# Later W_q loads and folds, earlier v tiles and warming on a constant in a fused attention and GEGLU kernel

## The chip, the cores and the metric

The kernel runs on one core of one Trainium2 chip. The metric is the time of the device for one execution, in microseconds (us); the median of several runs is given with the lowest and the highest. TensorE is PE, its weight loads are PEld, VectorE is DVE, ScalarE is ACT, GpSimd is POOL, and SyncE is SP, which issues all DMA transfers of this kernel. Each engine works through its own queue in order.

## What is computed

Two blocks follow each other on one sequence of 2048 rows of width 640. The first is linear attention with 32 heads of width 20 and a learned feature map; the second is a gated feed-forward layer of width 1536. Cut to what matters:

```python
x = A_x                                     # (1, 2048, 640), bf16
qkv = layernorm(x) @ wqkv                   # q, k, v: 32 heads of 20
pq, pk = q @ w_phi[h], k @ w_phi[h]         # per head, 20 x 20
phi_q = concat(softmax(pq), softmax(-pq))   # 40 features
phi_k = concat(softmax(pk), softmax(-pk))
kv, z = phi_k.T @ v, sum(phi_k)
o = (phi_q @ kv) / (phi_q @ z + 1e-6)
h = x + o @ wo
out = h + (gelu(layernorm(h) @ w_gate) * (layernorm(h) @ w_up)) @ w_down
```

## The kernel before

The 2048 rows are 16 tiles of 128 rows, in four blocks of four (`x_sb[0]` to `x_sb[3]`). The width of 640 is five chunks of 128 (`NC`). The order of every engine's instructions is written out by hand; the program's order is the queue's order.

**Folding.** `w_phi` is multiplied into W_k and W_q once, so that k and q come out of the projections ready for the exponentials. W_k and W_q are loaded transposed (`load_T`, five DMA transposes each, line 187, into `WkT` and `WqT`). `bd` builds `BD`, a block-diagonal form of `w_phi`, from the tile `wphi` and a mask on DVE (line 389). `fold` (lines 215 to 240) multiplies one 128-row chunk after the other, six matmuls each (tile `wa`), and copies each result out of PSUM: by ACT where the chunk is in `KA` (for W_k) or `QA` (for W_q), otherwise by DVE.

**Layernorm.** `ln_st` takes a tile's statistics on DVE (line 110); the reciprocal standard deviation comes from ACT (tiles 0 to 2, `log=True`) or from POOL (lines 122 and 123). `ln_ap` applies it on DVE or ACT. The result must be transposed into `LN1T`: with `on_pe` by five PE transposes and a copy out of PSUM by ACT or DVE (`ln_tp`, line 148), otherwise by a DMA transpose on SP's queue (line 150). Tiles 0 and 1 are only centred at first (`ln_0`, tile `xc`), and their scale is applied when v and k are read out; their full layernorm is made up for at tile 10 of the loop. Tile 3's statistics are two ACT passes with running sums (`st3_act`) and five small POOL steps.

**Start.** `warm` runs matmuls on a zeroed tile (line 211) while the first loads are on their way: nine of 512 columns, and two more behind the first transposes. Then v of tiles 0 to 2 is built in pieces (`v_part`, line 291), as the chunks of W_v land; the folds of W_k, v of tile 3 and the transposes of tiles 3 and 4 follow.

**Loop over the tiles t.** `k_tile` does k's ten matmuls (line 275, 320 columns each) and two exponentials on ACT (tile `E`, line 308). Until the end of the tiles, `v_mm(t + 4)` and `v_ev(t + 4)` do v of four tiles on, `ln_ap(t + 6)` the layernorm of six tiles on, and `k_norm` sums, inverts and scales on DVE and POOL (tiles `sk`, `rs`, `vt`). `kv_tile` (line 341) adds phi_k.T @ v of finished tiles into one PSUM tile, in the groups of `KVG`. `FQ` says at which t each chunk of W_q is folded. At t = 15 the q projection begins (`q_mm`, line 363), and from there attention, the output projection and the feed-forward layer run with q's remaining work between them.

**PSUM.** The big tiles (`gtile`) share four buffers of two banks; from t = `T3` there are three, the fourth goes to `kvp`.

Of the kernel before, what the change touches and what calls it, by code (L numbers as in the profile page):

```python
# [8 lines left out]
BF16 = mybir.dt.bfloat16  # L9
F32 = mybir.dt.float32  # L10
ALU = mybir.AluOpType
ACTF = mybir.ActivationFunctionType
# [5 lines left out]
def kernel(  # L18
# [12 lines left out]
    nc = tc.nc  # L31
    P = 128
    S = 2048
    D = 640
# [3 lines left out]
    NT = S // P  # L38
    NB = NT // 4
    NC = D // P  # L40
    NF = FF // P
    EPS = 1e-5
    HD = D // 2

    H0 = [(P * c) // Dh for c in range(NC)]
    NH = [(P * c + P - 1) // Dh - H0[c] + 1 for c in range(NC)]
    NWARM = 9
    VP = (0, 2, 4, 6, 9, 11)
    KA, QA = (1,3), (0,1,2,3,4)
    FQ = (4, 5, 6, 7, 8)  # L50

    QG = ((0, 1), (2, 3), (4, 5), (6,), (7, 8), (9, 10), (11, 12), (13, 14), (15,), (16,), (17,), (18,), (19,))
    QT = (15, 15, 15, 15)
    WA = 2
    T3 = 4

    KVG = {5: (0, 1), 9: (2, 3, 4, 5), 13: (6, 7, 8, 9), 15: (10, 11)}
    VC = Dh + 1
# [6 lines left out]
    x_v = A_x.rearrange("b (p t) d -> p (b t) d", t=NT)  # L65
# [23 lines left out]
    nhalf = const.tile([P, 2], F32, name="nhalf")  # L89
# [10 lines left out]
    def gtile(name):  # L100
        return psG.tile([P, 2, 512], F32, name=name, tag="G")
# [74 lines left out]
    nc.sync.dma_start(Wv[:, 0:2, :], w_v[:, 0:2, 2 * D:3 * D])  # L176
    nc.sync.dma_start(x_sb[0][:, 2:3, :], x_v[:, 2:3, :])
    nc.sync.dma_start(Wv[:, 2:4, :], w_v[:, 2:4, 2 * D:3 * D])
    nc.sync.dma_start(wphi, phi_v.rearrange("(c p) f -> p c f", p=P))
    nc.sync.dma_start(Wv[:, 4:5, :], w_v[:, 4:5, 2 * D:3 * D])  # L180
    nc.sync.dma_start(x_sb[0][:, 3:4, :], x_v[:, 3:4, :])
    nc.sync.dma_start(x_sb[1][:, 0:2, :], x_v[:, 4:6, :])

    def load_T(WT, i, *ds):

        for d in ds:
            nc.sync.dma_start_transpose(WT[:, :, d * P:(d + 1) * P], A_wqkv[d * P:(d + 1) * P, i * D:(i + 1) * D])  # L187
# [4 lines left out]
    wu_v = B_w_up.rearrange("(c p) n -> p c n", p=P)  # L192


    zero = fp.tile([P, 512], BF16, name="zero")
    nc.vector.memset(zero, 0.0)
    for i in range(8):
        nc.vector.memset(vS[i][:, :, Dh], 1.0)
    make_identity(nc, ident)
# [6 lines left out]
                                compare_op=ALU.is_ge, fill=0.0, base=Dh - 1 - off, channel_multiplier=-1)  # L206

    wu = gtile("wu")
    def warm(n):
        for _ in range(n):  # L210
            nc.tensor.matmul(wu[:, 0, :], lhsT=zero[:, 0:P], rhs=zero, start=True, stop=True)

    warm(NWARM)

    def fold(WT, W2, halves, ds=range(NC)):

# [37 lines left out]
    def ln_st(*tiles, act=True, between=None, log=False):  # L254
        for t, v in zip(tiles, ln_stats(p1, [x_sb[t // 4][:, t % 4, :] for t in tiles], "1", act, between, log)):
            lnp[t] = v

    def ln_ap(t, on_act=False, on_pe=False):
        ln = (ln_act if on_act else ln_dve)(p1, "1", *lnp[t])
        if on_pe:  # L260
            lnp[t] = ln
        else:
            transpose_to(LN1T[t // 4][:, :, t % 4 * P:(t % 4 + 1) * P], ln, False)

    def ln_tp(t, on_dve=False):
        transpose_to(LN1T[t // 4][:, :, t % 4 * P:(t % 4 + 1) * P], lnp[t], True, on_dve)

    def lnT(t, c):
        b, tl = divmod(t, 4)
        return LN1T[b][:, c, tl * P:(tl + 1) * P]  # L270

    def proj(ps, t, W, us=(0, 1)):
        for u in us:
            for c in range(NC):
                nc.tensor.matmul(ps[:, u, 0:HD], lhsT=lnT(t, c), rhs=W[:, c, u * HD:(u + 1) * HD],  # L275
                                 start=(c == 0), stop=(c == NC - 1))

    pv = {}

    def v_mm(t, us=(0, 1)):  # L280
        if 0 in us:
            pv[t] = gtile("pv")
        proj(pv[t], t, Wv, us)

    def v_part(t, *cs):

        if 0 in cs:
            pv[t] = gtile("pv")
        for c in cs:
            for u in range(2):  # L290
                nc.tensor.matmul(pv[t][:, u, 0:HD], lhsT=lnT(t, c), rhs=Wv[:, c, u * HD:(u + 1) * HD],
                                 start=(c == 0), stop=(c == NC - 1))

    def v_ev(t):
        nc.scalar.activation(vS[t % 8][:, :, 0:Dh].rearrange("p (u h) f -> p u h f", u=2),
                             pv[t][:, :, 0:HD].rearrange("p u (h f) -> p u h f", f=Dh), ACTF.Copy,
                             scale=lnp[t][2] if t in CT else 1.0)
# [4 lines left out]

    def k_tile(t):
        pk = gtile("pk")
        proj(pk, t, Wk2)
        Ek[t] = ev.tile([P, 2, D], BF16, name="E", bufs=8)
        for s in range(2):
            nc.scalar.activation(Ek[t][:, s, :].rearrange("p (u f) -> p u f", u=2), pk[:, :, 0:HD],  # L308
                                 ACTF.Exp, scale=((lnp[t][2], nrstd[t]) if t in CT else (1.0, -1.0))[s])
# [60 lines left out]
    def st3_act(i):  # L370

        xt = x_sb[0][:, 3, :]
        nc.scalar.activation(sq3, xt, (ACTF.Square, ACTF.Identity)[i], accum_out=sm3[:, i:i + 1])
        if i == 1:
            nc.gpsimd.tensor_scalar(v3[:, 0:1], sm3[:, 1:2], sm3[:, 1:2], -1.0 / (D * D), op0=ALU.mult, op1=ALU.mult)
            nc.gpsimd.tensor_scalar_add(v3[:, 0:1], v3[:, 0:1], EPS)
            nc.gpsimd.tensor_scalar(v3[:, 1:2], sm3[:, 0:1], 1.0 / D, v3[:, 0:1], op0=ALU.mult, op1=ALU.add)
            nc.gpsimd.tensor_tensor(v3[:, 2:3], v3[:, 1:2], nhalf[:, 0:1], op=ALU.pow)
            nc.gpsimd.tensor_scalar(v3[:, 3:4], sm3[:, 1:2], 1.0 / D, None, op0=ALU.mult)
            lnp[3] = xt, v3[:, 3:4], v3[:, 2:3], None  # L380

    sq3 = fp.tile([P, D], BF16, name="sq3")
    sm3 = fp.tile([P, 2], F32, name="sm3")
    v3 = fp.tile([P, 4], F32, name="v3")

    def bd(c0, c1):

        n = c1 - c0
        nc.vector.tensor_tensor(BD[:, c0:c1], wphi[:, c0:c1, None, :].to_broadcast([P, n, 8, Dh]),
                                hmask[:, c0:c1, :, None].to_broadcast([P, n, 8, Dh]), ALU.mult)  # L390
# [4 lines left out]
    xc = [ln_0(t) for t in CT[:1]]  # L395
    tr_c(0)
    xc.append(ln_0(1))
    warm(WA)
    ln_st(2, act=False, log=True)
    v_part(0, 0, 1)  # L400
    tr_c(1)
    st3_act(0)
    v_part(0, 2, 3)
    bd(0, 3)
    ln_ap(2, on_pe=True)
    bd(3, NC)
    st3_act(1)
    v_part(1, 0, 1, 2, 3)
    ln_tp(2, True)
    v_part(0, 4)  # L410
    v_ev(0)
    ln_st(4, act=False)
    ln_ap(3, on_pe=True)
    v_part(1, 4)
    v_ev(1)
    v_part(2, *range(NC))
    v_ev(2)
    nc.sync.dma_start(x_sb[1][:, 2:4, :], x_v[:, 6:8, :])
    nc.sync.dma_start(x_sb[2], x_v[:, 8:12, :])
    nc.sync.dma_start(x_sb[3], x_v[:, 12:16, :])  # L420
    fold(WkT, Wk2, False, (0, 1, 2))
    ln_tp(3, False)
    fold(WkT, Wk2, False, (3, 4))
    v_mm(3)
    v_ev(3)
    ln_ap(4, on_pe=True)
    ln_tp(4)
    ln_st(5, act=False)
    ln_st(6)
    ln_ap(5, on_pe=True)  # L430
    ln_st(7)
    fp_cm.__exit__(None, None, None)
    ev_cm = tc.tile_pool(name="ev", bufs=1, side="right", reuse_waits="tile")
# [2 lines left out]
    for t in range(NT):  # L436
        if t == T3:
            ps_cm.close()
            psG = ps_cm.enter_context(tc.tile_pool(name="psG", bufs=3, space=PSUM, reuse_waits="tile"))
            psK = ps_cm.enter_context(tc.tile_pool(name="psK", bufs=1, space=PSUM, reuse_waits="tile"))  # L440
            kvp = psK.tile([P, 2, 512], F32, name="kvp")
        k_tile(t)
        if t == 0:
            ln_ap(6)
        if t in FQ:
            fold(WqT, Wq2, True, [i for i, f in enumerate(FQ) if f == t])
        for j in range(len(QT)):
            if t == QT[j]:
                q_mm(j)
                q_exp(j)  # L450
        for i in KVG.get(t, ()):
            kv_tile(i)
        if t + 4 < NT:
            v_mm(t + 4)
            if t == 0:
                ln_tp(5)
        if t > 0 and t + 6 < NT:
            ln_ap(t + 6, on_act=True)
        if t + 4 < NT:
            v_ev(t + 4)  # L460
        if t % 2 == 0 and t + 8 < NT:
            ln_st(t + 8, t + 9)
        k_norm(t)
        if t < NC:
            load_T(WqT, 0, t)
        if t == 10:

            for i in CT:
                ln_ap(i)
        if t == 9:  # L470
            nc.gpsimd.memset(KV, 0.0)
            nc.gpsimd.memset(kmask, 1.0)
            for r in HALF:
                nc.gpsimd.affine_select(out=kmask[r], in_=kmask[r], pattern=[[4, NC], [-Dh, 4]],
                                        compare_op=ALU.is_ge, fill=0.0, base=0, channel_multiplier=1)
                nc.gpsimd.affine_select(out=kmask[r], in_=kmask[r], pattern=[[-4, NC], [Dh, 4]],
                                        compare_op=ALU.is_ge, fill=0.0, base=Dh - 1, channel_multiplier=-1)
            nc.gpsimd.tensor_copy(KV[:, :, 0, :, KC - 1], kmask)
            nc.gpsimd.tensor_copy(KV[:, :, 1, :, 0], kmask)
        if t == 10:  # L480
            nc.sync.dma_start(Wg, wg_v)
            nc.sync.dma_start(Wo, wo_v)
            nc.sync.dma_start(Wu, wu_v)
# [328 lines left out]
```

## Time and profile before

| | |
|---|---|
| median of 3 runs | 278.56 us (277.83 to 278.84) |
| the profiled execution | 278.98 us |
| its span, first to last instruction | 277.1 us |
| PE busy | 271.7 us (98%) |
| DVE busy | 176.5 us (64%) |
| ACT busy | 138.9 us (50%) |
| POOL busy | 97.0 us (35%) |

The profile is one execution. All times in it count from the start of the span; the execution's own time is 1.9 us longer than the span. A row of the timeline is: start, time from the first start to the last end, engine, line, operation, what it writes and reads with sizes, how many instructions, and in square brackets how long the engine was idle before and what ended that. A busy PE isn't one at its peak: matmuls are pipelined, and the ends in the profile are modelled.

### The profile page before, as it was taken

What the parts mean: (1) busy time and instruction counts of PE and PEld (TensorE: products, weight loads), DVE (VectorE), ACT (ScalarE), POOL (GpSimd) and SP (SyncE); (2) the same over time, 40 slices, a digit from 0 to 9 for tenths busy, and PEclk for the clock granted to TensorE, in tenths of its full rate; (3) what the DMA queues carried; (4) which work ended last, traced back from release to release, by engine and by line L of the source; (5) the groups of instructions that cost most, each with busy time, mean ns of one, the idle gap of its engine ahead of it and who ended that gap; (6) DMA issues with size and microseconds to landing.
All of it is one profiled execution on the core that took longest, in us unless ns stands there. A gap on an engine that the chain in (4) does not pass through costs nothing.

```text
span 277.1 us, 5913 instructions
## 1 busy us (share of the span) xinstructions
PE 271.7 (98%) x2337; PEld 173.2 (62%) x2337; DVE 176.5 (64%) x337; ACT 138.9 (50%) x239; POOL 97.0 (35%) x221
## 2 busy tenths in 40 slices
PE   8999999999999999999999999999999999999995
PEld 3677777774655887788864555675555577444574
DVE  6699999899396786576467773346876433332322
ACT  4679989668597846365543354313245410223100
POOL 4337997774302216455403463102165300000000
PEclk9999999999999999999999999999999999999999
DMA  6964842289740021314111123110123211000011
GB/s 198 184 241 102 109 78 50 26 229 393 251 151 0 4 47 26 72 47 97 28 50 47 25 50 71 25 55 21 47 47 70 27 47 47 27 0 0 0 50 47
DMA packets 42235, 21.37 MB, mean 77 GB/s; under 512 B 35040, under 2 KB 40416, under 8 KB 42208
## 3 DMA queue, kind: packets, MB, share of 16 engines
q1 hardware_dynamic: 42208, 21.01, 30.8%
q8 instruction: 18, 0.29, 0.4%
q14 instruction: 9, 0.07, 0.1%
HBM read 10.18 MB, written 2.62 MB: 46 GB/s over the span
## 4 chain that ended last, share of the span: by engine, by line
PE 87%; SPq 4%; DMA 3%; DVE 2%; ACT 2%; issue 1%
PE gu L657 38%; PE pd L676 19%; PE pq L363 8%; PE po L600 8%; PE pk L275 5%; PE pv L275 4%; PE ab L528 3%; SPq L187 2%; PE kvp L341 2%; DMA LN1T<-ln 2%; DVE stats L110 1%; DMA WkT<-in_A_wqkv_dram 1%; ACT E L308 1%; ACT ln L134 1%; PE wa L229 1%
## 5 line engine op out<-in xcount | busy, mean ns | idle before, releaser
L660 ACT ACTIVATE g<-gu 128x512 bf16<-128x512 f32 (+1 forms) x60 | 30.7, 512 | 69.1 <-PE gu L657 68.2
L663 DVE TENSOR_TENSOR GT<-gu,g 128x512 bf16<-128x512 f32 (+1 forms) x60 | 34.3, 579 | 48.2 <-PE gu L657 39.3
L657 PE MATMUL gu<-LN2T,Wg 128*128 128x512 bf16 (+1 forms) x300 | 61.8, 337 | 0.1
L657 PE MATMUL gu<-LN2T,Wu 128*128 128x512 bf16 (+1 forms) x300 | 61.7, 336 | 0.0
L676 PE MATMUL pd<-Wd,GT 128*128 128x320 bf16 (+2 forms) x396 | 53.5, 295 | 0.0
L676 PEld LDWEIGHTS <-GT 128*128 128x128 bf16 x396 | 37.9, 98 | 14.7 <-DVE GT L663 0.2
L657 PEld LDWEIGHTS <-Wu 128*128 128x128 bf16 x300 | 29.4, 98 | 22.6
L657 PEld LDWEIGHTS <-Wg 128*128 128x128 bf16 x300 | 28.8, 98 | 21.4
L275 PEld LDWEIGHTS <-LN1T 128*128 128x128 bf16 x290 | 27.9, 98 | 10.9 <-DMA LN1T<-ln 0.3
L679 DVE TENSOR_TENSOR y<-pd,x_sb 128x320 bf16<-128x320 f32 (+2 forms) x29 | 13.9, 480 | 29.0 <-PE pd L676 29.0
L323 POOL TENSOR_TENSOR vt<-vS,rs 128x672 bf16<-128x672 bf16 x22 | 29.1, 1343 | 9.1 <-DVE rs L319 7.4
L600 PE MATMUL po<-Wo,oT 128*128 128x320 bf16 x160 | 24.4, 299 | 0.0
L275 PE MATMUL pk<-Wk,LN1T 128*128 128x320 bf16 x160 | 24.0, 299 | 0.0
L315 DVE TENSOR_REDUCE sk<-E 128x64 f32<-128x1280 bf16 x16 | 22.9, 1434 | 1.2 <-ACT E L308 1.2
L363 PE MATMUL pq<-LN1T,Wq 128*128 128x512 bf16 x100 | 22.9, 379 | 0.0
L368 ACT ACTIVATE Eq<-pq 128x1024 bf16<-128x1024 f32 (+1 forms) x26 | 19.9, 830 | 2.4 <-PE pq L363 2.4
L308 ACT ACTIVATE E<-pk 128x640 bf16<-128x640 f32 x28 | 18.3, 716 | 4.5 <-PE pk L275 4.3
L600 PEld LDWEIGHTS <-oT 128*128 128x128 bf16 x160 | 15.6, 98 | 7.4 <-ACT oT L148 0.3
L275 PE MATMUL pv<-Wv,LN1T 128*128 128x320 bf16 x130 | 19.8, 299 | 0.2 <-DMA LN1T<-ln 0.2
L577 DVE TENSOR_TENSOR tt<-AB,w 128x1280 bf16<-128x1280 f32 x12 | 17.9, 1488 | 1.1 <-POOL w L570 0.9
L134 ACT ACTIVATE ln<-x_sb,v,rstd 128x640 bf16<-128x640 bf16 x14 | 12.9, 920 | 10.7 <-POOL v L636 10.3
L363 PEld LDWEIGHTS <-Wq 128*128 128x128 bf16 x100 | 9.5, 98 | 10.4 <-issue 0.2
(112 smaller groups left out, 292.8 us busy)
## 6 DMA issues: line engine op xcount, KB each, us to landing
out_dram<-y SPq DMA_DIRECT2D x15, 160.0 KB, 1.8
Wg<-in_B_w_gate_dram SPq DMA_DIRECT2D x1, 1920.0 KB, 9.1
Wu<-in_B_w_up_dram SPq DMA_DIRECT2D x1, 1920.0 KB, 15.0
Wd<-in_B_w_down_dram SPq DMA_DIRECT2D x1, 1920.0 KB, 8.0
x_sb<-in_A_x_dram SPq DMA_DIRECT2D x2, 640.0 KB, 6.6
Wo<-in_A_wo_dram SPq DMA_DIRECT2D x1, 800.0 KB, 10.7
x_sb<-in_A_x_dram SPq DMA_DIRECT2D x4, 160.0 KB, 2.9
Wv<-in_A_wqkv_dram SPq DMA_DIRECT2D x2, 320.0 KB, 3.8
```

Of the source, the lines that this page charges most:

```text
L275: nc.tensor.matmul(ps[:, u, 0:HD], lhsT=lnT(t, c), rhs=W[:, c, u * HD:(u + 1) * HD], start=(c == 0), stop=(c == NC - 1))
L308: nc.scalar.activation(Ek[t][:, s, :].rearrange("p (u f) -> p u f", u=2), pk[:, :, 0:HD], ACTF.Exp, scale=((lnp[t][2], nrstd[t]) if t in C ...
L315: nc.vector.reduce_sum(sk, Ek[t].rearrange("p s (h f) -> p (s h) f", f=Dh), axis=AX.X)
L323: eng.tensor_tensor(vt[:, s], vS[t % 8], rs[:, s * H:(s + 1) * H, None].to_broadcast([P, H, VC]), ALU.mult)
L363: nc.tensor.matmul(pqs[j][:, i, :], lhsT=Wq2[:, kc, c * P:(c + 1) * P], rhs=LN1T[b][:, kc, :], start=(kc == 0), stop=(kc == NC - 1))
L368: nc.scalar.activation(Eq[j][:, :, s, :], pqs[j][:, 0:len(QG[j])], ACTF.Exp, scale=(1.0, -1.0)[s])
L577: nc.vector.tensor_tensor(tt.rearrange("p s (h f) -> p s h f", f=Dh), num, w[:, :, :, None].to_broadcast([P, 2, H, Dh]), ALU.mult)
L600: nc.tensor.matmul(pos[u], lhsT=st[t][:, c, :], rhs=Wo[:, c, u * HD:(u + 1) * HD], start=(c == 0), stop=(c == NC - 1))
L657: nc.tensor.matmul(gu[i][:, 0:n], lhsT=W[:, c, f * P:(f + 1) * P], rhs=LN2T[b][:, c, a0:a1], start=(c == 0), stop=(c == NC - 1))
L660: nc.scalar.activation(g[:, 0:n], gu[0][:, 0:n], ACTF.Gelu_apprx_tanh)
L663: nc.vector.tensor_tensor(st[b, "g", f][:, a0:a1], gu[1][:, 0:n], g[:, 0:n], ALU.mult)
L676: nc.tensor.matmul(ps, lhsT=st[b, "g", f][:, tl * P:(tl + 1) * P], rhs=Wd[:, f, f0:f1], start=(f == 0), stop=(f == NF - 1))
```

## The change

- Warming reads the constant 1.0 that the framework provides (a broadcast of one column) in place of a zeroed tile, so the memset goes. In front: seven matmuls of 512 columns and eight of 128 in place of nine of 512. Behind the first transposes: seven of 128 in place of two of 512.
- The load of tile 3's x stands ahead of `wphi` and of W_v's last chunk on SP's queue.
- `BD` is built in one piece, behind the layernorm of tile 2.
- Tile 3's statistics are the mean first and then the squares of the centred values; two POOL steps are left of five. Its layernorm (`ln_3`) stands behind the statistics of tile 4.
- The transposes of tiles 3 and 4 are copied out by DVE; those of tile 3 come ahead of the folds of W_k. v of tile 3 stands ahead of fold 3, v of tile 4 ahead of fold 4. ACT copies the chunks 0, 2 and 4 of W_k (before: 1 and 3).
- k of tile 0 takes the row chunks in the outer loop and the halves in the inner one.
- W_q is loaded at t = 7 to 10 in place of 0 to 4 and folded at t = 10 to 14 in place of 4 to 8.
- Three PSUM buffers from t = 3 in place of 4. The loads of Wg, Wo and Wu stand at t = 13 in the program in place of 10.

```diff
-    NWARM = 9
-    KA, QA = (1,3), (0,1,2,3,4)
-    FQ = (4, 5, 6, 7, 8)
+    KA, QA = (0, 2, 4), (0, 1, 2, 3, 4)
+    LQ = (7, 8, 9, 9, 10)
+    FQ = (10, 11, 12, 13, 14)
-    WA = 2
-    T3 = 4
+    T3 = 3
...
     nc.sync.dma_start(Wv[:, 2:4, :], w_v[:, 2:4, 2 * D:3 * D])
+    nc.sync.dma_start(x_sb[0][:, 3:4, :], x_v[:, 3:4, :])
     nc.sync.dma_start(wphi, phi_v.rearrange("(c p) f -> p c f", p=P))
     nc.sync.dma_start(Wv[:, 4:5, :], w_v[:, 4:5, 2 * D:3 * D])
-    nc.sync.dma_start(x_sb[0][:, 3:4, :], x_v[:, 3:4, :])
...
-    zero = fp.tile([P, 512], BF16, name="zero")
-    nc.vector.memset(zero, 0.0)
+    ones = nc.const_aps.tensor(1.0, [P, 512], BF16)
...
-    def warm(n):
-        for _ in range(n):
-            nc.tensor.matmul(wu[:, 0, :], lhsT=zero[:, 0:P], rhs=zero, start=True, stop=True)
-    warm(NWARM)
+    def warm(*cols):
+        for n in cols:
+            nc.tensor.matmul(wu[:, 0, 0:n], lhsT=ones[:, 0:P], rhs=ones[:, 0:n], start=True, stop=True)
+    warm(*[512] * 7, *[P] * 8)
...
-    def proj(ps, t, W, us=(0, 1)):
-        for u in us:
-            for c in range(NC):
+    def proj(ps, t, W, us=(0, 1), rows=False):
+        for u, c in sorted(((u, c) for u in us for c in range(NC)), key=lambda x: x[::-1] if rows else x):
...
-        proj(pk, t, Wk2)
+        proj(pk, t, Wk2, rows=t == 0)
...
-        nc.scalar.activation(sq3, xt, (ACTF.Square, ACTF.Identity)[i], accum_out=sm3[:, i:i + 1])
-        if i == 1:
...
+        if i == 0:
+            nc.scalar.activation(sq3, xt, ACTF.Identity, scale=-1.0 / D, accum_out=v3[:, 0:1])
+        else:
+            nc.scalar.activation(sq3, xt, ACTF.Square, bias=v3[:, 0:1], accum_out=v3[:, 1:2])
+            nc.gpsimd.tensor_scalar(v3[:, 2:3], v3[:, 1:2], 1.0 / D, EPS, op0=ALU.mult, op1=ALU.add)
+            nc.gpsimd.tensor_tensor(v3[:, 3:4], v3[:, 2:3], nhalf[:, 0:1], op=ALU.pow)
+
+    def ln_3():
+        ln = lnp[3] = p1.tile([P, D], BF16, name="ln1", bufs=3)
+        nc.vector.tensor_scalar(ln, x_sb[0][:, 3, :], v3[:, 0:1], v3[:, 3:4], op0=ALU.add, op1=ALU.mult)
...
-    warm(WA)
+    warm(*[P] * 7)
     ln_st(2, act=False, log=True)
     v_part(0, 0, 1)
     tr_c(1)
     st3_act(0)
     v_part(0, 2, 3)
-    bd(0, 3)
     ln_ap(2, on_pe=True)
-    bd(3, NC)
+    bd(0, NC)
     st3_act(1)
-    v_part(1, 0, 1, 2, 3)
+    v_part(1, 0, 1)
     ln_tp(2, True)
+    v_part(1, 2, 3)
     v_part(0, 4)
     v_ev(0)
-    ln_st(4, act=False)
-    ln_ap(3, on_pe=True)
     v_part(1, 4)
     v_ev(1)
+    ln_st(4, act=False)
+    ln_3()
+    ln_ap(4, on_pe=True)
     v_part(2, *range(NC))
     v_ev(2)
...
+    gtile('wu')
+    ln_tp(3, True)
     fold(WkT, Wk2, False, (0, 1, 2))
-    ln_tp(3, False)
-    fold(WkT, Wk2, False, (3, 4))
+    ln_tp(4, True)
     v_mm(3)
+    ln_st(5, act=False)
     v_ev(3)
-    ln_ap(4, on_pe=True)
-    ln_tp(4)
-    ln_st(5, act=False)
+    fold(WkT, Wk2, False, (3,))
+    v_mm(4)
+    ln_ap(5, on_pe=True)
+    fold(WkT, Wk2, False, (4,))
+    v_ev(4)
+    ln_tp(5)
     ln_st(6)
-    ln_ap(5, on_pe=True)
     ln_st(7)
...
-        if t + 4 < NT:
+        if 0 < t < NT - 4:
             v_mm(t + 4)
-            if t == 0:
-                ln_tp(5)
...
-        if t < NC:
-            load_T(WqT, 0, t)
+        load_T(WqT, 0, *[i for i, f in enumerate(LQ) if f == t])
...
-        if t == 10:
+        if t == 13:
             nc.sync.dma_start(Wg, wg_v)
```

## The prediction

> **What bounds the kernel now.** I read the page first, then the chain of waits in order of time, then the timeline of the first 70 us, engine by engine.
>
> ```profile
> span 277.1 us, 5913 instructions
> PE 271.7 (98%) x2337; PEld 173.2 (62%) x2337; DVE 176.5 (64%) x337; ACT 138.9 (50%) x239; POOL 97.0 (35%) x221
> PE 87%; SPq 4%; DMA 3%; DVE 2%; ACT 2%; issue 1%
> ```
>
> TensorE (PE) is the bound, and the change takes no real matmul away: the same projections, folds and transposes are in the program, only the warming differs. So all it can win is time in which PE waits. The chain shows where that is:
>
> ```profile
> 11.21 3.41 DMA WkT<-in_A_wqkv_dram
> 14.67 0.50 PE wa L229 x6
> ...
> 28.85 4.90 DMA LN1T<-ln
> 33.80 1.53 PE pv L275 x10
> 35.33 1.36 PE pk L275 x10
> 36.69 0.32 PE wa L229 x6
> ```
>
> After 33.80 us the chain is nearly all PE, to the end of the span. Before it, loads, VectorE (DVE) and ScalarE (ACT) take turns. The prices are in the chain too: ten 320-column matmuls (one v or k tile) 1.36 us, one fold 0.32, five transposes 0.28 (rows at 79.63 and 83.61). The timeline shows the start:
>
> ```profile
> 0.92 0.27 DVE L196 MEMSET zero<- 128x256 uint32 x1 [0.92 <-PEq L796]
> 1.25 4.02 PE L211 MATMUL wu<-zero 128*128 128x512 bf16 x9 [1.25 <-DVE zero L196]
> 4.22 0.39 DVE L251 TENSOR_SCALAR xc<-x_sb,mvc 128x640 bf16<-128x640 bf16 x1
> 5.06 0.74 PE L147 MATMUL tp<-ident,xc 128*128 128x128 bf16 x5
> ...
> 9.23 0.74 ACT L373 ACTIVATE sq<-x_sb 128x640 bf16<-128x640 bf16 x1 [1.56 <-DMA x_sb<-in_A_x_dram]
> 12.85 0.45 DVE L139 TENSOR_SCALAR ln<-x_sb,v 128x640 bf16<-128x640 bf16 x1 [1.58 <-POOL v L379]
> 16.73 1.52 PE L275 MATMUL pk<-Wk,LN1T 128*128 128x320 bf16 x10
> 19.44 0.44 PE L147 MATMUL tp<-ident,ln 128*128 128x128 bf16 x5
> ```
>
> The first tile, ready at 4.61, waits for warming until 5.06. ACT waits 1.56 us for x of tile 3; DVE, in order, waits 1.58 for GpSimd's (POOL's) chain on it. In the transposes, PE finishes at 19.72 (19.44 + 0.28) the following work: six tile transposes, five folds, v of tiles 0 to 4, k of tile 0. That is my yardstick.
>
> **Part by part: the start.** Warming on a constant: PE need not wait for the memset; ACT and DVE begin at 0.79 and 0.92, so PE at about 0.85 instead of 1.24. Nine matmuls in 4.02 us, less a tail of 0.18, are 427 ns each; a 128-column one is a quarter, 107. 7 x 0.427 + 8 x 0.107 = 3.85, so it ends at 4.70, and the first transposes come 0.36 earlier. Alone this wins nothing: the next wait is further down. The seven small ones behind them (0.75) end before ACT's copy, as the two big ones did (6.51 against 6.58).
>
> Loads: the DMA answers put the landings at 6.9 us (Wv chunks 2-3, L178), 8.07 (wphi, L179), 8.8 (Wv chunk 4, L180), 9.25 (x of tile 3, L181) and 10.0 (tiles 4-5, L182). x of tile 3 took 0.45 of the queue. Moved ahead of wphi it lands near 7.4, wphi near 8.55, Wv's chunk near 9.3; tiles 4-5, and the W_k transposes behind them on SP's queue, do not move.
>
> DVE: copy of tile 1 ends about 7.85, the layernorm of tile 2 now comes at once (to 8.32), then the whole BD when wphi is there: 0.66 + 0.48 less one overhead, 1.02, to 9.6. The copy of tile 2 is queued behind BD and ends at 10.14 (before: 9.74 + 0.49 = 10.23). So wphi's later landing eats the earlier start.
>
> Tile 3: ACT's two sums can start at 7.7 instead of 9.23 and end at 9.56. POOL's five steps (11.02 to 12.82) become two (0.27 and 0.57 with a gap), rstd at 10.6. DVE does the statistics of tile 4 first, to 11.27, and tile 3's layernorm from 11.3 to 11.75 instead of 12.85 to 13.30. Its wait of 1.58 is gone; a wait of 0.5 for tile 4's rstd comes in its place, with the copy of tile 3 queued behind it (12.73 to 13.22).
>
> PE then, in its new order: v of tile 2 from 10.2 to 11.56; transposes of tile 3 at 11.80; folds 0 to 2 to 13.04; transposes of tile 4 at 13.27 (a PSUM buffer must come free); v of tile 3 13.55 to 14.91; fold 3 to 15.23 (its weights landed at 13.8); v of tile 4 to 16.59; fold 4 to 16.91 (landed at 14.6, so that wait is covered); transposes of tile 5 wait for DVE until 17.10, to 17.38; k of tile 0 to 18.74. By row chunks it asks for the last W_k chunk after eight matmuls, at 18.47, when ACT has long copied it (17.8). Without that order it would wait 0.3. Against 19.72: **0.98 us**. Evacuating chunks 0, 2 and 4 on ACT instead of 1 and 3 gives DVE 0.78 back, its two extra transpose copies take 0.98; in sum DVE reaches the end of tile 6's statistics at 18.16 instead of 18.88.
>
> **Part by part: the loop.** W_q's loads leave tiles 0 to 4 and its folds leave tiles 4 to 8. There ACT is full:
>
> ```profile
> 39.89 1.31 ACT L308 ACTIVATE E<-pk 128x640 bf16<-128x640 f32 x2
> 40.07 1.52 PE L275 MATMUL pv<-Wv,LN1T 128*128 128x320 bf16 x10
> 41.05 0.73 ACT L238 CAST Wq<-wa 128x640 bf16<-128x640 f32 x1
> ```
>
> The E rows start 3.15 apart (36.73, 39.89, 43.03, 46.18), PE's matmuls need 2 x 1.36 + 0.32 = 3.04, and PE loses 0.19 at 39.88, 0.15 at 43.10, 0.09 at 45.96, and 0.17 at 33.63 to a transposed tile that landed 4.9 us after issue instead of the usual 2.6. Without the fold's copy (0.58 from its start at 41.05 to that of ACT's next row at 41.63) ACT needs 2.57 against PE's 2.72. **0.60 us** come back, if nothing takes their place. What could: (a) transposed tiles. ACT's ln ends about 2.2 after a k tile, landing 2.65 later; PE wants it at 5.44: 0.6 of room. (b) The W_q loads stand on SP's queue between the layernorm transposes of tiles 13 to 15 and those of tiles 0 and 1; at 1.28 each to issue and 3 to 4.6 to land, the last is there about 54, its fold at about 58. (c) The folds at tiles 10 to 14 meet an ACT without layernorms there: 1.2 + 0.6 against PE's 1.68, with room from the kv matmuls. (d) The first q matmuls follow the last fold by one k tile; its copy is done at about 60.1, wanted at 60.66. (e) Wg, Wo and Wu stand later in the program, but nothing is between on SP's queue and they wait for nothing, so they go out where they did. (f) Three PSUM buffers from tile 3 on: E of the tile before is read 1 us before its buffer is wanted. I cost (a) to (f) at nothing; bounds 0 and 0.3 in sum, from PE's stalls of 0.1 to 0.2 in the rows above.
>
> The chain that must keep up is k_norm's, DVE and POOL:
>
> ```profile
> 51.96 1.49 DVE L315 TENSOR_REDUCE sk<-E 128x64 f32<-128x1280 bf16 x1 [1.22 <-ACT E L308]
> 68.99 1.96 POOL L323 TENSOR_TENSOR vt<-vS,rs 128x672 bf16<-128x672 bf16 x1 [1.35 <-DVE rs L319]
> 69.34 2.48 PE L341 MATMUL kvp<-vt,E 128*64 128x84 bf16 x120
> ```
>
> POOL's last vt ends at 70.95; PE wants it five sixths into its six kv tiles, at 71.4. DVE is full from 20 to 50, then waits 1.22 for E of tile 10. With folds gone from the tiles before, that E comes over 3 us earlier, so the wait goes: 0.72 + 1.22 = 1.94 earlier for DVE, 1.58 for PE. It keeps up, by 0.8.
>
> **Sum.** 0.98 + 0.60 = 1.58 us. The profiled execution took 278.98, its span 277.1 and 1.9 around it; it would become 277.4. It lies 0.42 above the median of 278.56, so the median becomes 277.0. The start is worth 0.5 (wphi delayed by its own 1.17 instead of 0.45) to 1.3 (tiles 4-5 usable at 10.0, no buffer wait); the loop 0.3 to 0.9 (all of PE's gaps between 19.72 and 61.70: 41.05 us of matmuls in 41.98). So this case spans 0.8 to 2.2.
>
> The clock is the unknown. The warm rows run at 427 ns per 512 columns, and 512-column matmuls in steady state take 4.32/20 = 216: PE is at half speed until some point between 5.5 and 6.6.
>
> The Trainium skill (TensorE: Matmul & The Clock Gate, Part 1) says that the clock is released by a window of about 3.4 us of sustained activity that runs free of the kernel's start, and Part 4 that transposes do not count as activity in the same way. That speaks against replacing 1024 columns of warming behind the first transposes by 896. By it one window missed would cost up to half of 3.4, 1.7 us, where my sum has zero.
>
> **Rivals.** *The k_norm chain does not move* (DVE's early savings are lost): POOL ends at 70.95 less the 1.22, 69.7, and PE, there at 69.8, hardly waits; if the 1.22 is lost too, PE waits until 70.95 and keeps about 0.5: 278.1. For it: DVE at 97% from 15 to 50. Against: the wait of 1.22 is PE's doing.
>
> *The start is taken back*: BD, now one piece ahead of tile 2's copy on DVE, holds up every later copy; only the loop's 0.6 stays: 278.0. For it: wphi landed 4.9 after issue, the slowest per byte.
>
> *Slower: PE stays at half speed.* At half speed until a time t, PE loses half of what lies between 6.2 (its first v matmul) and t, less the 1.3 us that it idles between 6.2 and 10.2 in my schedule: (t - 6.2)/2 - 1.3. The 1.58 are gone at t = 12.0; from 14.7 the kernel is slower by over 0.5%; at 17, all of the start, 4.1 are lost against 1.58 won: 281.1. For it: less warming, and small pieces. Against: PE's gaps after 6.2 are hardly more than before, when it was at full speed from 6.6.
>
> *The change does not do what it says* for the weights' loads, (e) above, and that costs nothing either way.
>
> **Chances.** Forecast 0.66 (own range 276.4 to 277.8), the k_norm chain 0.12, the start taken back 0.12, slower 0.10. A measurement of this kernel tells 0.5%, 1.39 us, from no change. Below 277.17 lie four fifths of the forecast case: 0.52; above 279.95 0.10; the rest 0.38. The range runs from 276.0, the 276.4 with a little more from a clock released earlier, to 278.5, past the two middle rivals and a half-speed period.
>
> **What would show it.** Right: first transposes near 4.7; tile 3's layernorm near 11.3; k of tile 0 ends before 19; no PE gaps between tiles 4 and 9; DVE without a wait at tile 10; q matmuls from near 60.1. Wrong: tile 2's copy later than 10.5, v matmuls at 270 ns after 7 us, PE waiting for vt at the last kv tiles, for W_q's last copy, or for a transposed tile.

## The result and the profile after

The changed kernel takes 277.56 us (277.19 to 278.45), the kernel before, run beside it, 278.57 (277.76 to 279.19). The ratio is 0.9973, with a 95% interval of 0.9961 to 0.9986. So it is faster: by 1.0 us between the medians, by 0.75 (0.4 to 1.1) by the ratio. The forecast was 277.0, a gain of 1.6; half to two thirds of it came. The executions of the kernel before gather near 278.0 and near 278.8 us, 99 of the 171 of this study at 278.3 or more, so its median depends on how many fall into each group. The profiled execution of the changed kernel took 277.38 us.

The first lines of the page of the changed kernel and its shares of the chain by engine:

```profile
span 275.7 us, 5930 instructions
PE 269.6 (98%) x2335; PEld 173.7 (63%) x2348; DVE 177.5 (64%) x336; ACT 138.3 (50%) x238; POOL 96.4 (35%) x218
PE 88%; ACT 4%; DVE 3%; DMA 2%; issue 1%; POOL 0%
```

PE is still the bound, and less of the chain is waiting. The chain of waits in order of time (start, us, what), at the start and at the only late transposed tile on it:

```profile
8.14 0.98 DVE BD L388
...
12.63 0.44 PE tp L146 x5
13.06 1.36 PE pv L272 x10
14.42 0.32 PE wa L227 x6
14.74 1.36 PE pv L272 x10
16.10 0.33 PE wa L227 x6
...
27.09 4.32 DMA LN1T<-ln
31.46 1.53 PE pv L272 x10
```

The five rows from 12.63 to 16.43 are the new order at work: v of tiles 3 and 4 stand where PE waited for W_k's loads. The last two rows are the same trouble as in the kernel before, with the same tile: there 4.90 us from 28.85, here 4.32 from 27.09.

The timeline of the changed kernel, in the columns that were explained above:

```profile
0.83 3.72 PE L209 MATMUL wu<-const-bfloat16-1.0 128*128 128x512 bf16 x15 [0.83 <-PEq L797]
4.73 0.45 PE L146 MATMUL tp<-ident,xc 128*128 128x128 bf16 x5 [0.18 <-DVE xc L249]
8.68 0.83 ACT L373 ACTIVATE sq<-x_sb,v 128x640 bf16<-128x640 bf16 x1
10.56 0.46 DVE L380 TENSOR_SCALAR ln<-x_sb,v 128x640 bf16<-128x640 bf16 x1
31.46 1.53 PE L272 MATMUL pv<-Wv,LN1T 128*128 128x320 bf16 x10 [0.30 <-DMA LN1T<-ln]
67.65 1.97 POOL L320 TENSOR_TENSOR vt<-vS,rs 128x672 bf16<-128x672 bf16 x1 [1.35 <-PE pq L360]
272.52 0.29 DVE L680 TENSOR_TENSOR y<-pd,x_sb 128x128 bf16<-128x128 f32 x1 [0.31 <-PE pd L677]
```

The first transposes come at 4.73 in place of 5.06, tile 3's layernorm at 10.56 in place of 12.85 and without the wait of 1.58 before it. Of PE's waits in the loop the row at 31.46 shows the larger one, 0.30 us. POOL's last `vt` ends at 69.62 in place of 70.95, and it is PE's q matmuls that it waited for.

A second wait for a transposed tile doesn't show as idle time, since the modelled ends of the matmuls cover it:

```profile
38.26 1.52 PE L272 MATMUL pk<-Wk,LN1T 128*128 128x320 bf16 x10
39.78 1.53 PE L272 MATMUL pv<-Wv,LN1T 128*128 128x320 bf16 x10
```

These rows start 1.52 us apart, where a k tile otherwise takes 1.36: 0.16 more. The trace has tile 12's transpose issued at 36.52 and landed at 39.73, after 3.2 us.

**Where the gain lies.** Four marks divide the two profiled executions: the first k matmul of tile 1 (it follows k of tile 0), the first q matmul, the end of the last `y`, the last instruction.

| stretch, us | before | after | gain |
|---|---|---|---|
| to k of tile 1 | 19.72 | 17.88 | 1.84 |
| k of tile 1 to the first q matmul | 41.97 | 41.93 | 0.04 |
| first q matmul to the last y | 212.89 | 213.00 | -0.11 |
| last y to the last instruction | 2.56 | 2.86 | -0.30 |

The start gave all of it, the loop nothing, and 0.30 were lost behind the last `y`. The 0.11 between the first q matmul and the last `y` stand also in x3_late, dve_shift and wphi_act (213.07 to 213.10); their cause is open. The profiled execution of before lay 0.42 above its median and that of after 0.18 below, so the medians show less than these rows. The third W_k transpose took 2.00 us to issue in that execution of before, 1.27 in that of after.

### The profile page after: what moved, and what is told of

Its sections match the earlier page's. It is cut to its first block, busy times and chain, and to the rows that moved or that the text cites. A ratio compares the mean times of both kernels' runs of the same rounds, so it can differ in the third digit from the quotient of the medians.

```text
span 275.7 us, 5930 instructions
## 1 busy us (share of the span) xinstructions
PE 269.6 (98%) x2335; PEld 173.7 (63%) x2348; DVE 177.5 (64%) x336; ACT 138.3 (50%) x238; POOL 96.4 (35%) x218
## 4 chain that ended last, share of the span: by engine, by line
PE 88%; ACT 4%; DVE 3%; DMA 2%; issue 1%; POOL 0%
PE gu L658 38%; PE pd L677 19%; PE pq L360 8%; PE po L601 8%; PE pk L272 5%; PE pv L272 5%; PE ab L529 3%; PE kvp L338 2%; ACT E L305 2%; DMA LN1T<-ln 2%; ACT ln L133 1%; DMA x_sb<-in_A_x_dram 1%; PE wa L227 1%; DVE statsc L109 1%; DVE stats L109 1%
## 5 line engine op out<-in xcount | busy, mean ns | idle before, releaser
L320 POOL TENSOR_TENSOR vt<-vS,rs 128x672 bf16<-128x672 bf16 x22 | 29.1, 1344 | 9.1 <-DVE rs L316 7.4
```

Source lines behind the costliest of these rows:

```text
L320: eng.tensor_tensor(vt[:, s], vS[t % 8], rs[:, s * H:(s + 1) * H, None].to_broadcast([P, H, VC]), ALU.mult)
```

## The experiments

Ratios are against the kernel before, run beside each kernel on the same chip. Its medians there were 278.05 to 278.75, so the ratios compare better than the medians, which come from several chips. Single executions of one kernel spread by 0.5 to 1.7 us, those of warm_7_0 and warm_7_0_dve by 2.4 and 2.8, so a tenth in a median decides little, and the marks of the profiles are read with it. Each row has 12 executions, dve_shift and warm_zero_t4 have 6, the changed kernel 15.

| run | us, median | ratio, 95% interval |
|---|---|---|
| the changed kernel | 277.56 | 0.9973 (0.9961 to 0.9986) |
| wq_early | 277.69 | 0.9975 (0.9965 to 0.9985) |
| wq_later | 278.13 | 0.9986 (0.9973 to 0.9998) |
| x3_late | 278.38 | 0.9991 (0.9978 to 1.0003) |
| folds_first | 278.05 | 0.9988 (0.9978 to 0.9999) |
| wphi_act | 277.71 | 0.9972 (0.9961 to 0.9983) |
| warm_9_2 | 277.70 | 0.9969 (0.9959 to 0.9980) |
| warm_zero | 279.20 | 1.0027 (1.0016 to 1.0039) |
| warm_zero_t4 | 277.62 | 0.9958 (0.9942 to 0.9974) |
| fetch_gap | 278.77 | 1.0004 (0.9992 to 1.0016) |
| fetch_mid | 278.57 | 1.0018 (1.0006 to 1.0031) |
| wq_early_shift | 277.59 | 0.9978 (0.9967 to 0.9989) |
| dve_shift | 277.32 | 0.9955 (0.9938 to 0.9972) |
| fetch_gap_dve | 278.61 | 1.0004 (0.9993 to 1.0016) |
| fetch_mid_dve | 278.34 | 1.0006 (0.9995 to 1.0016) |
| warm_7_0 | 280.14 | 1.0047 (1.0033 to 1.0062) |
| warm_7_0_dve | 279.99 | 1.0052 (1.0029 to 1.0076) |
| warm_7_0_t4 | 278.79 | 1.0014 (0.9999 to 1.0028) |

### Which half brings the gain

**wq_early**: the changes of the start alone.

```diff
-    LQ = (7, 8, 9, 9, 10)
-    FQ = (10, 11, 12, 13, 14)
+    LQ = (0, 1, 2, 3, 4)
+    FQ = (4, 5, 6, 7, 8)
-    T3 = 3
+    T3 = 4
```

> The changed kernel with W_q's loads and folds back at tiles 0 to 4 and 4 to 8 and four PSUM buffers up to tile 4: only the new start is left. Theory (the prediction's terms hold): 0.98 us under the kernel before, near 277.6. Rival (part of the 0.98 is a late W_k transpose that only some executions of the kernel before show: its third one took 2.0 us to issue in the profiled execution and 1.28 otherwise): the median is 0.2 to 0.5 under the kernel before, near 278.2.

**wq_later**: the kernel before with W_q's loads at t = 7 to 10 and its folds at 10 to 14, nothing else.

> The kernel before with nothing changed but W_q's loads (tiles 7 to 10) and folds (tiles 10 to 14). Theory: 0.6 us under the kernel before, near 278.0, and no gap of PE between tiles 4 and 9 except at the kv matmuls. Rival (ACT and the transposed tiles find other waits): 0.0 to 0.3.

The start alone takes 277.69, W_q alone 278.13. The interval of the ratio leaves W_q alone 0.06 to 0.75 us. In the loop stretch (k of tile 1 to the first q matmul) the profiles show 41.74 for W_q alone (41.97 before) and 42.50 for the start alone: with tiles that start earlier, ACT's full queue and a tile that landed late (tile 12, 0.46 us of waiting) cost more than they did. In this stretch moving W_q is worth 0.23 us on the old start and 0.57 on the new one; 0.16 of the 0.57 is that the late tile cost 0.46 there and 0.30 in the changed kernel. The new start by itself lost 0.53 in the loop. In the time the 0.57 hardly show (277.69 against 277.56, ratios 0.9975 and 0.9973): behind the last `y` the changed kernel takes 2.86, the start alone 2.63.

**before_again**: the kernel before, one more profile.

> The kernel before once more, for a second profile. If the W_k transposes issue in 5 x 1.28 us this time, the last W_k chunk lands near 13.9 instead of 14.6, k of tile 0 starts near 16.0 instead of 16.7, and the execution takes about 277.9; if one takes 2.0 again, as in the first profile, 278.6 to 279.0.

It took 277.89. Its third W_k transpose needed 1.28 us to issue and not 2.00, and k of tile 1 came at 18.71 in place of 19.72. Against this execution the changed start gains 0.83, against the other 1.84. Over all profiles here that issue took 1.27 to 2.22; what makes it late isn't settled.

### The parts of the start

**x3_late**: the load of tile 3's x back behind W_v's last chunk.

```diff
-    nc.sync.dma_start(x_sb[0][:, 3:4, :], x_v[:, 3:4, :])
     nc.sync.dma_start(wphi, phi_v.rearrange("(c p) f -> p c f", p=P))
     nc.sync.dma_start(Wv[:, 4:5, :], w_v[:, 4:5, 2 * D:3 * D])
+    nc.sync.dma_start(x_sb[0][:, 3:4, :], x_v[:, 3:4, :])
```

> After, with only the load of tile 3's x put back behind W_v's last chunk. Theory (the prediction's working, where that load lets ACT's statistics, and with them tile 3's layernorm, come early): x of tile 3 lands near 9.2 in place of 7.3, the layernorm of tile 3 about 1 us later than 10.56, PE loses 0.3 to 0.6 at the start, 277.8 to 278.2. Rival (DVE's order, with BD and tile 4's statistics ahead of it, sets tile 3's layernorm): less than 0.2 lost, 277.5 to 277.75.

The timeline of this kernel:

```profile
9.10 0.74 ACT L371 ACTIVATE sq<-x_sb 128x640 bf16<-128x640 bf16 x1 [1.28 <-DMA x_sb<-in_A_x_dram]
11.84 0.45 DVE L380 TENSOR_SCALAR ln<-x_sb,v 128x640 bf16<-128x640 bf16 x1 [0.81 <-POOL v L375]
12.34 0.45 PE L146 MATMUL tp<-ident,ln 128*128 128x128 bf16 x5 [1.09 <-DVE ln L380]
```

ACT waits 1.28 us for x again, tile 3's layernorm comes 1.28 later, PE waits 1.09 for it, and the median is 0.8 above the changed kernel's; by the ratios it is 0.5, inside the 0.3 to 0.6 that the theory gave. So the load's place is a working part of the start. The profiled execution also had a slow third W_k transpose (1.83 to issue), so its marks may overstate the loss.

**folds_first**: folds 3 and 4 ahead of v of tiles 3 and 4.

```diff
-    v_mm(3)
...
-    v_ev(3)
...
-    v_mm(4)
...
+    v_mm(3)
+    v_ev(3)
+    v_mm(4)
```

> The changed kernel with folds 3 and 4 of W_k ahead of v of tiles 3 and 4 again (their statistics and layernorm in the same order). Theory (the order covers the landing of the last two W_k chunks): PE waits for the last chunk, landing at 13.8 to 14.6, 0.5 us in an execution with five transposes of 1.28 and up to 1.2 with a late one; so 0.4 to 0.9 over the changed kernel, near 278.2. Rival (DVE's layernorm of tile 5 ends last anyway): within 0.2.

0.5 us are lost (0.4 by the ratios): k of tile 0 starts at 17.45 in place of 16.52. The order covers the landing of the last W_k chunks.

**wphi_act**: `wphi` issued by ACT ahead of everything, so that it is off SP's queue.

```diff
+    nc.scalar.dma_start(wphi, phi_v.rearrange("(c p) f -> p c f", p=P))
...
-    nc.sync.dma_start(wphi, phi_v.rearrange("(c p) f -> p c f", p=P))
```

> The changed kernel with wphi's load issued by ACT ahead of its table load instead of by SP. Theory (the third W_k transpose issues late, 1.73 to 2.2 us instead of 1.28, where wphi's 25 KB in pieces of 40 bytes are still on the DMA engines): it issues in 1.28, the loads behind land 0.4 to 0.8 earlier, BD no longer waits for wphi, and the kernel is 0.3 to 0.8 under the changed one with fewer executions at the upper end. Rival (the late transpose has another cause, and the start is bound by DVE): the third issue stays between 1.3 and 2.2 and the time is the changed kernel's, 277.5.

It landed at 3.60 in place of 8.01 and nothing became faster (277.71), and the third W_k transpose was again slow to issue (1.61). Neither the place of `wphi` nor its load bounds the start.

**warm_9_2** and **warm_zero**: the old amounts of warming, nine and two matmuls of 512 columns, once on the constant, once on the zeroed tile with its memset.

```diff
-    ones = nc.const_aps.tensor(1.0, [P, 512], BF16)
+    ones = fp.tile([P, 512], BF16, name="zero")
+    nc.vector.memset(ones, 0.0)
-    warm(*[512] * 7, *[P] * 8)
+    warm(*[512] * 9)
...
-    warm(*[P] * 7)
+    warm(*[512] * 2)
```

> The changed kernel with its warming cut as in the kernel before, still on the constant: nine matmuls of 512 columns in front (the same 4608 columns in all) and two behind, eleven matmuls fewer. Theory (a transposed tile lands late when a 16 KB piece of PE's program is fetched while it is in flight, and the fetch comes after a fixed number of PE instructions): 22 PE instructions fewer put the fetch of 28.25 us some 1.5 us later, tile 9's transpose (issued at 27.1) lands after 2.6 us instead of 4.3, PE's gap of 0.30 us before v of tile 9 goes, and another transfer is late instead; 0 to 0.3 us under the changed kernel. Rival (the lateness has to do with the tile or the time, not the fetch): tile 9 lands after 4.3 again.

> The changed kernel with the old warming altogether: a zeroed tile (with its memset on DVE), nine matmuls of 512 columns and two. Theory (warming on the constant brings PE forward by 0.4, but the next wait is further down): same as warm_9_2 within 0.2, first transposes at 5.0 instead of 4.7. Rival (the earlier start carries through): 0.3 to 0.4 slower than warm_9_2.

The shapes don't matter (277.70 against 277.56). The fetch part of the first expectation missed: a fetch of program (next section) came at 29.42, 1.2 us later, and met tile 9 all the same, which landed after 4.54 us and cost PE 0.52. The zeroed tile looked 1.5 us dearer, but its timeline has the loss elsewhere, at k of tile 3 (the expectation below says tile 4):

```profile
25.04 0.78 ACT L293 ACTIVATE vS<-pv 128x640 bf16<-128x640 f32 x1
25.86 1.52 PE L273 MATMUL pk<-Wk,LN1T 128*128 128x320 bf16 x10 [1.64 <-ACT vS L293]
```

k of tile 3 shares no data with that v tile, tile 6; what they can share is a PSUM buffer. **warm_zero_t4** keeps four buffers until t = 4:

```diff
-    T3 = 3
+    T3 = 4
```

> The earlier kernel of after with the old warming on a zeroed tile took 279.2, 1.5 more than the same warming on the constant, and its PE waited 1.64 us at k of tile 4 for ACT's copy of a v tile. Here four PSUM buffers are kept until t = 4, as in the kernel before, all else as in that kernel. Theory (the wait is for a PSUM buffer, of which three are left from t = 3): the wait of 1.64 goes and the time is 277.5 to 278.0. Rival (the old warming costs the time in another way, by a later or slower start of PE): 278.9 to 279.4, whatever the buffers do.

277.62, and no such wait. So the old warming costs nothing by itself; with it, three buffers from tile 3 on make k wait for the v tile just finished. That is a hazard which the prediction's point (f) had costed at nothing; the changed kernel has three buffers too, and it did not strike in its own order. Why some orders of the start wake it is open.

### The late transposed tile

The trace has every DMA packet, and the page calls one queue "instruction": it brings 18 packets of 16 KB in each execution, fetches of program. The twenty traces hold 800 DMA transposes of layernorms and attention outputs. Of the 660 that no such fetch overlaps between issue and landing, none took over 3.50 us, and 611 took at most 2.75. All 61 that took over 3.50 had one under way; of the 53 where it started 0.9 to 2.3 us after their issue, 50 are among these, and the median of the 53 is 4.26. In the changed kernel's trace such a fetch starts at 28.26 and takes 1.52. (Tile 12's 3.2 us are among the 49 between 2.75 and 3.50 without a fetch; their cause is open.) The DMA answers for two windows of 3 and 6 us (40 slices each, tenths of the 16 engines busy), first tile 8, then tiles 9 and 10:

```profile
DMA  0000000000000001599999999951000000000000
```

```profile
DMA  0000000089999900000000045059999800000000
```

Tile 8's packets run in one piece. Those of tile 9 start at 28.2, stop at 29.1 and end only at 30.7, in slices hardly busy: in the trace, packets resume at 29.76, where the 16 KB packet ends, singly and some 0.03 us apart, as of one engine, and 18 other packets stand open for 1.5 to 1.8 us meanwhile. The rest follow at 30.5. Tile 10's follow at 31. The loads of W_q are at neither place.

The Trainium skill (Runtime: NRT & Kernel Launch, Instruction fetch mechanics) says that an engine's program is refilled over a DMA queue in blocks of 16 KiB, 256 instructions, and that a block's cost is mostly hidden. The 18 packets of 16 KB fit the size: PE and PEld have 2335 + 2348 = 4,683 instructions here, 18.3 times 256. Hidden it is for PE's own instructions, which have no gap while the fetch runs from 28.26 to 29.78, but not for the transpose that it meets.

**fetch_gap** and **fetch_mid** move the fetch by more, smaller warming matmuls of the same 4608 columns:

```diff
-    warm(*[512] * 7, *[P] * 8)
+    warm(*[512] * 5, *[P] * 16)    # fetch_gap
+    warm(*[512] * 6, *[P] * 12)    # fetch_mid
```

> After, with warming of the same 4608 columns in 5 matmuls of 512 and 16 of 128 (7 and 8 before), so six more matmuls stand ahead of everything on PE. In the trace of after, the transposed layernorm of tile 9 took 4.32 us to land where its neighbours take 2.6, and a 16 KB fetch of program started 2 us after its issue; PE waited 0.30 us for it at 31.16. Theory (the late tiles are those that a fetch of PE's program meets on the DMA engines): the fetch comes some 0.7 us earlier, between the two tiles that it could meet, tile 9 lands in 2.6 to 2.9 us, the wait of 0.30 goes, and the time is 0.1 to 0.3 under after (277.2 to 277.4). Rival (the late landing has another cause at this place, such as the loads of W_q): tile 9 again takes over 4 us and the time is that of after.

> After, with warming of 6 matmuls of 512 and 12 of 128 (7 and 8 before; the same columns, three matmuls more ahead of everything). With six more, the 16 KB fetch of PE's program moved from 28.25 to 26.72 us, met tile 8 (landing 4.26 us after issue in place of 2.60), let tile 9 go (2.58), and PE waited 1.25 us there. Theory (the place of the fetch against the transposes decides): with three more it begins near 27.5, when tile 8 has landed and tile 9 has been issued for less than 0.7 us; tile 9 lands in 2.6 to 3.4 us, PE waits for neither, first k matmul of tile 1 to first q matmul takes 41.5 to 41.7 in place of 41.93, and the time is 0.2 to 0.4 under after, 277.2 to 277.4. Rival (more small matmuls in front cost time in another way, or the transposes are late for another reason): 277.9 to 278.7, as with six more.

Both lost about 1 us (0.9 and 1.3 by the ratios), by the theory's mechanism and against its forecast. The fetch came at 26.72 and 26.66, 1.5 us earlier where 0.7 had been worked out, and met tile 8. PE wants tile 8 2.9 us after its issue, tile 9 4.1. The timeline of fetch_gap:

```profile
28.80 1.53 PE L272 MATMUL pv<-Wv,LN1T 128*128 128x320 bf16 x10 [1.25 <-DMA LN1T<-ln]
```

Tile 8 landed after 4.26 (fetch_mid: 4.36), tile 9 after 2.58 (2.57). The late landing goes with the fetch and not with the tile, and a fetch is worth nothing to 1.3 us according to the tile it meets. Three and six matmuls more put it at the same place, so it doesn't move with their number; by what it moves stays open.

**wq_early_shift**: wq_early with three matmuls fewer in front, `warm(*[512] * 8, *[P] * 4)`.

> The kernel with W_q at its early place and all changes of the start (277.7), with warming of 8 matmuls of 512 and 4 of 128 (7 and 8 there: three matmuls fewer ahead of everything). There a fetch of PE's program began 2.13 us after the issue of tile 12, which landed in 4.23, and PE waited 0.46 us for it. Theory (that wait is the fetch's, the rest of the loop's loss is ACT's full queue): the fetch begins some 0.5 later, when tile 12 has landed, the wait of 0.46 goes, first k matmul of tile 1 to first q matmul takes 42.0 to 42.1 in place of 42.50, and the time is 277.2 to 277.4; moving W_q is then worth 0.4 to 0.5 in that stretch against fetch_mid's. Rival (the early loads of W_q make the tile late): tile 12 again over 4 us, 277.6 to 277.8.

The fetch did not move (39.72 against 39.86), tile 12 again took 4.18, and the stretch 42.44. It tells nothing apart but shows again that a few matmuls don't set the fetch's place.

### The last instruction

**dve_shift**: four of DVE's memsets at the start are done twice.

```diff
-    for i in range(8):
+    for i in (0, 1, 2, 3, *range(8)):
         nc.vector.memset(vS[i][:, :, Dh], 1.0)
```

> The changed kernel with four more memsets on DVE in its idle time before the first x arrives (the same ones written twice): every later instruction of DVE stands four places further in its queue. Theory (the last DRAIN of DVE, 0.36 us late in the changed kernel's profile, waits for the fetch of the next piece of DVE's program): it comes without that delay, and the kernel is 0.3 to 0.4 under the changed one, near 277.2. Rival (the delay has another cause, or is one execution's chance): same as the changed kernel, 277.56.

In the trace of the changed kernel DVE's last DRAIN, the instruction that closes its program, begins 0.47 us after the start of the wait for a semaphore ahead of it, in that of before 0.11. With four instructions more on DVE it is 0.11 again, and the profiled execution ends 2.58 us behind its last `y` in place of 2.86. Three further kernels were run with and without the four memsets, **fetch_gap_dve**, **fetch_mid_dve** and **warm_7_0_dve**, each with 0.11 against 0.46 or 0.47. The step goes with the number of DVE's instructions in the trace: the nine kernels with 449, those that wait included, have it, and the eleven with 447, 448, 450 or 453 don't. What it is worth in the time is less sure than the 0.3 us in the traces. The medians are lower in all four pairs (0.24, 0.16, 0.23, 0.15), but the ratios only in two of them (dve_shift and fetch_mid_dve), and the intervals of every pair overlap.

> The two edits together: the warming of 5 matmuls of 512 and 16 of 128, and four repeated memsets on DVE at the start, which took DVE's last instruction from 0.47 us after its semaphore back to 0.11. Theory (two separate terms, one in a PE wait at tile 9, one behind the last y): they add, 0.4 to 0.7 under after, 276.8 to 277.1, and the last DVE instruction again starts 0.11 after its semaphore. Rival (neither is more than a drift between executions): 277.3 to 277.6.

> The same with four repeated memsets on DVE at the start, with which DVE's last instruction begins 0.11 us after its semaphore in place of 0.47. Theory: the two terms add, 0.4 to 0.7 under after, 276.9 to 277.2. Rival (the memsets alone gave 277.3 because the fetch happened to lie better in that run): no better than fetch_mid, 277.2 to 277.4.

The step came as expected; the times (278.61 and 278.34) missed, since the fetch met tile 8 in both.

### How much warming it needs

**warm_7_0**: seven warming matmuls of 512 and none of the fifteen small ones.

```diff
-    warm(*[512] * 7, *[P] * 8)
+    warm(*[512] * 7)
...
-    warm(*[P] * 7)
```

> After with seven warming matmuls of 512 columns in front and nothing else (8 of 128 in front and 7 of 128 behind the first transposes are gone). Fetch theory: with eleven matmuls fewer the fetch of PE's program began at 29.42, 2.09 us after tile 9's issue; with fifteen fewer it comes at 29.5 to 31. If it lands behind tile 9 (over 2.6 us after its issue) it can only meet tile 10, which PE wants 4.4 us after its issue and not 4.0: PE's wait in the loop goes to zero, first k matmul of tile 1 to first q matmul takes 41.5 to 41.7, and the time is 0.2 to 0.4 under after. If it still meets tile 9, that stretch stays at 41.9 to 42.1 and the time is 277.5 to 277.8. Clock rival: PE stays at half speed for longer; at half speed until 12 us all of the change's gain is gone, 278.5 or more.

> The same with four repeated memsets on DVE at the start, so that DVE's last instruction begins 0.11 us after its semaphore and not 0.47. Fetch and last instruction both out of the way: 0.5 to 0.7 under after, 276.8 to 277.1. If the fetch still meets tile 9, 277.2 to 277.5, as with the memsets alone. Clock rival: 278 or more.

These two took 280.14 and 279.99: the clock rival came true. The fetch still met tile 9 (4.43 and 4.34 us to landing), and k of tile 3 again waited for a PSUM buffer, 1.63 us.

**warm_7_0_t4**: warm_7_0 with `T3 = 4`, against the buffer wait.

> After with seven warming matmuls of 512 columns in front and none behind, and four PSUM buffers until tile 4. Clock theory: the wait of 1.63 us goes, what is left over after is the half-speed time at the start, which varied between 8.7 and 11.5 us in the two profiles with this warming and moved k of tile 0 by 0.85 and 2.1 us: 278.2 to 279.2, with a spread between runs of over 2 us. Rival (the loss was the buffer's, the late clock is hidden behind loads): 277.5 to 277.9, a spread of 1 us.

Short warming with four buffers costs 1.2 us against the changed kernel (278.79; 1.1 by the ratios). Its first v tiles, in the timeline:

```profile
6.25 1.25 PE L288 MATMUL pv<-Wv,LN1T 128*128 128x320 bf16 x4 [0.78 <-ACT LN1T L147]
7.82 2.15 PE L288 MATMUL pv<-Wv,LN1T 128*128 128x320 bf16 x8
```

Eight matmuls in 2.15 us, 267 ns from start to start, where the changed kernel has 136 from its first v on. Half speed lasted until 9.6 us here and until 11.5 and 8.9 in the two others, though all three start alike; the page's row of the granted clock shows 9 throughout. So 3584 columns of warming in front (3.15 us) and none behind were too little in all three. With 4608 in front (3.4 to 4.0 us) and 896 or 1024 behind, as in all other kernels here, the v matmuls ran at full speed from 6.6 us at the latest in every profile. The two parts of the warming were not varied apart.

The Trainium skill (TensorE: Matmul & The Clock Gate, Part 1) has a window of some 3.4 us that runs free of the kernel's start. These runs agree with it as far as they go: the records of the granted clock, which 18 of the 20 traces have, begin full speed at 3.4 to 6.5 us with the full warming (in x3_late and the changed kernel at 3.5 and 4.1) and at 8.9 to 11.6 with the short one, each time spread by less than 3.4. They don't show its length.

## Why the prediction was right or wrong

- **The bound and the sign** were right: PE's waits at the start went, nothing took their place there.
- **The start, 0.98**: right in its mechanism, and between the two executions of before in its size (0.83 and 1.84). Each step came earlier than worked out: BD from 8.14 to 9.12 where 9.6 was worked out for its end, tile 2's copy until 9.53 and not 10.14, since `wphi` landed at 8.01 and not 8.55; tile 3's layernorm at 10.56 and not 11.3; k of tile 0 ended at 17.88 and not 18.74. The yardstick, 19.72, held a third W_k transpose of 2.00 us. wq_later, with the same start, had one of 2.22 (k of tile 1 at 19.80), before_again one of 1.28 (18.71); how often the kernel before has it isn't known. The changed start has k of tile 1 at 18.3 with one of 1.73 or 1.61 (dve_shift, wphi_act), so there it goes with a loss of 0.4, in the old start with one of 1.0.
- **The loop, 0.60: the step that failed.** It measured 0.04 in the profiled executions, and -0.06 against before_again (41.87). The term is the sum of four gaps, 0.19 + 0.15 + 0.09 + 0.17, with the points (a) to (f) costed at nothing. The first two, behind the folds, came back: the five folds take 1.67 us in place of 2.02, from start to start. So ACT did hold PE up there. The 0.09 ahead of the kv matmuls stands in every profile, of all kernels, and was not to be won. The 0.17 was taken for a stall that would go; it is the fetch of PE's program, it met tile 9 again, and cost 0.30. And tile 12 cost 0.16 that before doesn't have. 0.35 - 0.13 - 0.16 leaves 0.06. So it is point (a), 0.6 of room at a landing of 2.65, that was wrong: PE wants tile 8 2.9 us and tile 9 4.1 us after issue, and tiles 9 and 12 landed after 4.3 and 3.2. The upper bound, all of PE's time above 41.05 us of matmuls, was too high as well: the shortest stretch of any run is 41.57 (x3_late), 0.40 below before.
- **The sum, by luck**: it put the profiled execution at 277.4, and this one took 277.38. But the start gave 0.86 more than its term, the loop 0.56 less, 0.41 were lost behind the first q matmul, and 0.1 came from outside the span. The prediction then took the whole gain from one execution, 0.42 above its median, over to the median.
- **Costed at nothing, but not nothing**: DVE's last DRAIN, 0.30 behind the last y. No view of the profile names it, and the prediction's working ends before it.
- **k_norm's chain** kept up as worked out: no wait on DVE at tile 10, POOL's end 1.33 earlier. **Wg, Wo and Wu** went out right behind the transposes of tiles 0 and 1, as (e) said. **(f)** held in the changed order and failed in three others (1.63 to 1.64 us).
- **The slower rival** has its mechanism, seen with 1920 columns of warming fewer; the 128 fewer of the change weren't enough to wake it. Its price for half speed until 9.6 was too low, (9.6 - 6.2)/2 - 1.3 = 0.4, where warm_7_0_t4 lost 1.2: of the 1.3 us that PE should have idled between 6.2 and 10.2, the changed kernel's timeline has only 0.28 (at 7.25). With that the same formula gives 1.4.
- **The start is taken back** fell: k of tile 1 came 0.83 to 1.84 earlier, and wphi_act, where `wphi` landed at 3.60, was no faster than the changed kernel.

## What to carry to other kernels

Before a gap is counted as winnable, see which part of it any run has been without: a sum of matmul durations is not the floor. A transposed load that takes 4.3 us where its neighbours take 2.6 may have met a fetch of the program: look at the instruction queue's packets. More room for the loads of a tight loop, 2 us by these landings, looks safer than moving the fetch by the warming, by which no run here gained; no run tried the room. A yardstick from one execution should be checked against a second profile of the same kernel. A total that comes out right is checked term by term: here two wrong terms made it.

## What the runs showed of the hardware

- A 16 KB fetch of program takes 0.9 to 2.0 us. A DMA transpose in whose flight it starts, 0.9 to 2.3 us after the issue, landed after 3.6 to 4.9 us in 50 of 53 cases, where the usual is 2.6.
- When a few matmuls were added or removed far ahead of them, the fetches moved 1.5 us earlier with three and with six more, 0.1 with three fewer, and 1.2 later with eleven fewer.
- DVE's last DRAIN begins 0.11 or 0.47 us after the wait ahead of it: 0.47 in every kernel with 449 DVE instructions, 0.11 in all others. A boundary of program pieces would explain that; this was not shown.
- The lowest time of the study is dve_shift's, 277.32. A version with the fetch in a harmless place wasn't found.
